# One shared home for the last weight pieces and sixteen 8-byte loads at the end of the load queue: a decode step of attention plus MLP

## The chip, the cores and the metric

The kernel runs on one core of one Trainium2 chip. A core has TensorE (PE, matmuls), VectorE (DVE), ScalarE (ACT), GpSimd (POOL), SyncE (SP, which here only issues transfers) and 16 DMA engines that move data between device memory (HBM) and the core's on-chip memory (SBUF). SBUF has 128 partitions. The matmuls add up in a second on-chip memory, PSUM. A transfer is issued on the queue of an engine (here SP, ACT or POOL), carried out by DMA engines, and reports by a semaphore that it has landed.

The metric is device time in microseconds (us), the median over runs without the profiler. The profile shows one further execution. Its span, from the first to the last instruction, is a little shorter than the device time of that execution.

## The reference

One token `x` (1 × 1024) is normalised; attention with 32 query heads on 4 cached key/value heads of 65,536 positions each, and a small MLP, are added to it. All is bf16.

```python
def reference(A_x, A_k_cache, A_v_cache, A_wq, A_wo, B_x, B_w1, B_w2, B_w3, B_w4):
...
    x = A_x
    xn = _layernorm(x, axis=-1)
    return x + _A_ref(xn, A_k_cache, A_v_cache, A_wq, A_wo) + _B_ref(xn, B_w1, B_w2, B_w3, B_w4)
```

`_A_ref` is `softmax(q kᵀ / sqrt(128)) v`, projected by `wo` (4096 × 1024), with `q = xn wq` and `wq` 1024 × 4096. `_B_ref` normalises `xn` again and uses four weights: `h = gelu(layernorm(xn) w1)`, four quarters of `h` shifted along a sequence (which has one position here, so that the shifted values are all outside it), `x1 = xn + hs w2`, and `x1 + gelu(layernorm(x1) w3) w4`, where `w3` is 1024 × 3584 and `w4` 3584 × 1024. The two caches have 64 MiB each; the kernel reads 170 MB in all.

## The kernel before, in words

**Items.** All that is large is cut into 47 items (lines 82 to 91), each loaded by one transfer on SP's queue and used by one compute function. In order: `wq` in two halves; for each of four key/value heads `g` and each of four rounds `r` a tile of K and a tile of V (16,384 positions, 4 MiB each), with `w3` (two halves) and `w1` put in between, and `wo` of that head after its rounds; then `w2`; then `w4` in five pieces. `W4_PIECES` (line 19) is (16, 8, 2, 1, 1): 16, 8, 2, 1 and 1 of the 28 chunks of 128 rows that w4 has, so 4096, 2048, 512, 256 and 256 KB. In the text the five are called piece 0 to piece 4.

**Slots.** The pool `big` (line 61) holds five slots of 128 partitions × 32 KiB. `slot()` (line 95) takes the next one in rotation, so that an item lies where the item five places earlier lay, and its load waits until that item has landed and has been read for the last time. `issue` (line 98) takes a slot, picks the source and issues the load (line 118). `ensure` (line 129) issues items up to a number, and the main loop (lines 440 to 442) keeps the issues `LOOKAHEAD` = 4 items ahead of the computing. For the last items this means: piece 0 takes the slot of V of the last round but one, piece 1 that of K of the last round, piece 2 that of V of the last round, piece 3 that of the last `wo`, and piece 4 that of `w2`.

**Computing.** `compute_K` transposes a K tile in place on DVE (line 353), multiplies it with the queries on PE (line 357) and makes softmax weights of a round on DVE and ACT. `compute_V` multiplies the weights with the V tile on PE (line 389). `group_end` joins the four rounds of a head, and `compute_wo` projects the head. Everything that ends in the output is added up in one PSUM bank, `psB`, by `row_acc` (line 160): two rows of 512 sums, from `x`, `wo`, `w2` and `w4`.

**The end.** `compute_w4` (line 326) adds each piece to `psB`, two matmuls for each chunk: 32, 16, 4, 2 and 2. After the last piece ACT copies the first 256 columns of `psB` to SBUF (line 336) and DVE the other 256 (line 337); two stores of 1 KB each bring them to HBM, one on ACT's queue (line 339), one on SP's (line 340). Each engine issues its own instructions in the order of the program; when the instruction at the head waits, what is behind it waits too.

**Semaphores.** The framework gives each transfer that SP or ACT issues one of eight completion semaphores, in rotation over both queues. A transfer that takes a semaphore which an earlier transfer has used is issued only when that earlier transfer is known to have landed. The framework adds a wait in front of the issue where the program doesn't imply it anyway. At the end of the program SP waits for all eight.

Of the kernel before, what the change touches and what calls it, by code (L numbers as in the profile page):

```python
# [8 lines left out]
BF16 = mybir.dt.bfloat16  # L9
# [9 lines left out]
W4_PIECES = (16, 8, 2, 1, 1)  # L19
# [3 lines left out]
def kernel(  # L23
# [14 lines left out]
    nc = tc.nc  # L38
# [11 lines left out]
    NOUT = A_wo.shape[1]  # L50
# [8 lines left out]
    const = ctx.enter_context(tc.tile_pool(name="const", bufs=1))  # L59
# [20 lines left out]
    w4_start = [sum(W4_PIECES[:i]) for i in range(len(W4_PIECES))]  # L80

    items = [("wq", 0), ("wq", 1)]
# [10 lines left out]
    st = {}  # L93

    def slot():
        return big.tile([P, KEYS], BF16, name="slot")

    def issue(item):
        kind = item[0]
        t = slot()  # L100
        if kind == "wq":
            src = wq_v[:, 4 * item[1]:4 * item[1] + 4, :].rearrange("p c n -> p (c n)")
        elif kind == "w3":
            src = w3_v[:, 4 * item[1]:4 * item[1] + 4, :].rearrange("p c n -> p (c n)")
        elif kind == "w4":
            c0 = w4_start[item[1]]
            src = w4_v[:, c0:c0 + W4_PIECES[item[1]], :].rearrange("p c n -> p (c n)")
        elif kind == "w1":
            src = w1_v
        elif kind == "w2":  # L110
            src = w2_v
        elif kind == "wo":
            src = wo_v[item[1]]
        else:
            cache = A_k_cache if kind == "K" else A_v_cache
            _, g, r = item
            src = cache[0, g, r * KEYS:(r + 1) * KEYS, :].rearrange("(p k) d -> p (k d)", p=P)
        nc.sync.dma_start(out=t[:, 0:src.shape[-1]], in_=src)
        st[item] = t
# [7 lines left out]
    n_issued = [0]  # L127

    def ensure(upto):
        while n_issued[0] <= min(upto, len(items) - 1):  # L130
            issue(items[n_issued[0]])
            n_issued[0] += 1
# [85 lines left out]
    for cg in range(4):  # L218
        nc.vector.tensor_copy(out=selbig[:, cg, :].rearrange("p (hl dd) -> p hl dd", dd=16),
                              in_=sel32[:, 8 * cg:8 * cg + 8].unsqueeze(2).to_broadcast([P, 8, 16]))  # L220
    sel8big = const.tile([P, P], F32, name="sel8big")
    nc.vector.tensor_copy(out=sel8big[:].rearrange("p (hl dd) -> p hl dd", dd=16),
                          in_=sel8[:].unsqueeze(2).to_broadcast([P, 8, 16]))
# [3 lines left out]
    for b in range(2):  # L227
        for par in range(2):
            nc.vector.tensor_copy(out=psel[:, 2 * b + par, :].rearrange("p (a i) -> p a i", a=4),  # L229
                                  in_=iv[:, b, par, :].unsqueeze(1).to_broadcast([P, 4, 32]))  # L230
# [200 lines left out]
    def compute_wo(g):  # L431
        wt = st.pop(("wo", g))[:, 0:8 * NOUT].rearrange("p (j n) -> p j n", n=NOUT)
        oT5 = st.pop(("oT5", g))
        for j in range(8):
            for h2 in range(2):
                row_acc(h2, oT5[:, j:j + 1], wt[:, j, 512 * h2:512 * (h2 + 1)])

    compute = {"wq": compute_wq, "w3": compute_w3, "w1": compute_w1, "w2": compute_w2, "w4": compute_w4,
               "wo": compute_wo, "K": compute_K, "V": compute_V}
    for i, it in enumerate(items):  # L440
        ensure(i + LOOKAHEAD)
        compute[it[0]](*it[1:])


# [28 lines left out]
```

## Time and profile before

| what | value |
|---|---|
| median of 3 runs | 406.52 us (406.5 to 406.79) |
| the profiled execution, device time | 406.69 us |
| its span | 404.8 us |
| mean granted TensorE clock | 0.796 |
| PE busy | 245.7 us (61%) |
| DVE busy | 215.7 us (53%) |
| ACT busy | 37.7 us (9%) |
| read from HBM | 169.88 MB, 420 GB/s over the span |

The profile page divides the span into 40 equal slices and gives, as a digit in tenths, the busy share of each engine and of the 16 DMA engines together. Other views of the same trace list the instructions in order of time, what an engine waited for, the busy time in chosen stretches, the transfers with the time from issue to landing, and the chain of waits: from the last instruction back to what released it, and so on. A line such as `L118` is line 118 of the kernel. `SPq` and `ACTq` are the issuing instructions of SP and ACT; `PEld` is the loading of weights into PE. `x5` counts instructions, and `a<-b` says that `a` is written from `b`.

### The profile page before, as it was taken

What the parts mean: (1) busy time and instruction counts of PE and PEld (TensorE: products, weight loads), DVE (VectorE), ACT (ScalarE), POOL (GpSimd) and SP (SyncE); (2) the same over time, 40 slices, a digit from 0 to 9 for tenths busy, and PEclk for the clock granted to TensorE, in tenths of its full rate; (3) what the DMA queues carried; (4) which work ended last, traced back from release to release, by engine and by line L of the source; (5) the groups of instructions that cost most, each with busy time, mean ns of one, the idle gap of its engine ahead of it and who ended that gap; (6) DMA issues with size and microseconds to landing.
All of it is one profiled execution on the core that took longest, in us unless ns stands there. A gap on an engine that the chain in (4) does not pass through costs nothing.

```text
span 404.8 us, 3326 instructions
## 1 busy us (share of the span) xinstructions
PE 245.7 (61%) x1400; PEld 95.7 (24%) x1400; DVE 215.7 (53%) x235; ACT 37.7 (9%) x60; POOL 11.2 (3%) x30
## 2 busy tenths in 40 slices
PE   0385565328475847557657948384659474758456
PEld 0132222103132312112223313131233121213122
DVE  0419474017484848346665847475748383838500
ACT  0101101100201010120210010101010101010100
POOL 5001000000000000000010000000000000000000
PEclk9998878857795778768595868888958797679898
DMA  8999999999999999999999999999999999999993
GB/s 363 415 424 449 418 426 434 430 418 444 434 408 439 447 416 419 458 418 416 447 431 413 437 444 414 435 440 418 430 440 424 428 439 427 425 437 413 440 415 134
DMA packets 7065, 170.11 MB, mean 420 GB/s; under 512 B 1023, under 2 KB 1033, under 8 KB 1418
## 3 DMA queue, kind: packets, MB, share of 16 engines
q1 hardware_dynamic: 6772, 169.87, 98.0%
q8 instruction: 11, 0.18, 0.2%
q0 software_dynamic: 128, 0.02, 0.0%
q10 hardware_dynamic: 150, 0.01, 0.0%
q14 instruction: 4, 0.03, 0.0%
HBM read 169.88 MB, written 0.01 MB: 420 GB/s over the span
## 4 chain that ended last, share of the span: by engine, by line
DMA 54%; PE 23%; DVE 17%; ACT 2%; another core or an unknown queue 1%; issue 1%; DVEq 0%; ACTq 0%
DMA slot<-in_A_k_cache_dram 44%; DVE slot L353 11%; PE sc L357 10%; DMA slot<-in_B_w_dram 7%; PE psB L160 5%; PE oacc L389 4%; DMA x_bf<-in_A_x_dram 3%; DVE pT L377 2%; DVE mx L361 2%; ACT p_sb L374 2%; PE rows L244 1%; PE pm_e L417 1%; DVE m L365 0%; PE pm_mx L363 0%
## 5 line engine op out<-in xcount | busy, mean ns | idle before, releaser
L353 DVE STREAM_TRANSPOSE slot<-slot 128x2048 f32<-128x2048 f32 x64 | 142.3, 2281 | 61.1 <-DMA slot<-in_A_k_cache_dram 61.1
L357 PE MATMUL sc<-slot,qst 128*128 128x512 bf16 x512 | 131.6, 411 | 40.9 <-DVE slot L353 40.9
L389 PE MATMUL oacc<-slot,pT 128*32 128x512 bf16 x512 | 56.0, 616 | 48.0 <-DVE pT L377 48.0
L357 PEld LDWEIGHTS <-qst 128*128 128x128 bf16 x512 | 51.6, 103 | 125.1 <-issue 45.9
L361 DVE TENSOR_REDUCE mx<-sc 128x1 f32<-128x1024 f32 x16 | 19.6, 1225 | 34.7 <-PE sc L357 34.7
L374 ACT ACTIVATE p_sb<-sc,nball 128x1024 bf16<-128x1024 f32 x16 | 17.8, 1114 | 209.8 <-DVE nball L372 209.8
L389 PEld LDWEIGHTS <-pT 128*32 128x32 bf16 x512 | 17.5, 139 | 75.0 <-DVE pT L377 49.4
L377 DVE STREAM_TRANSPOSE pT<-p_sb 128x1024 bf16<-128x1024 bf16 x16 | 19.9, 1245 | 23.3 <-ACT p_sb L374 23.3
L244 PE MATMUL rows<-slot,xpad 128*32 128x512 bf16 (+1 forms) x144 | 13.6, 509 | 6.1 <-DMA slot<-in_B_w_dram 6.1
L363 PE MATMUL pm_mx<-ident_f,mx 128*1 128x128 f32 x16 | 4.3, 270 | 21.1 <-DVE mx L361 21.1
L160 PE MATMUL psB<-slot,oT 128*1 128x512 bf16 x64 | 12.6, 564 | 4.3 <-DVE oT L428 4.3
L394 ACT COPY ob<-oacc 128x512 f32<-128x512 f32 x12 | 7.0, 586 | 58.6 <-PE oacc L389 58.6
L160 PE MATMUL psB<-slot,dst_h 128*1 128x512 bf16 x56 | 7.9, 444 | 3.2 <-DMA slot<-in_B_w_dram 3.2
L370 PE MATMUL pm_mx<-ident_f,rep 1*128 1x1 f32 x16 | 3.5, 222 | 9.9 <-DVE rep L367 9.9
L417 PE MATMUL pm_e<-og,selbig 128*128 128x128 f32 x32 | 7.4, 403 | 3.4 <-DVE og L409 3.4
L244 PEld LDWEIGHTS <-xpad 128*32 128x32 bf16 x144 | 5.7, 127 | 15.0 <-issue 13.7
L172 PE MATMUL pm_ln<-ln_rowsum_a,ones_f 128*128 128x1 f32 x2 | 0.6, 348 | 13.6 <-DVE psel L229 13.6
L337 DVE CAST out<-psB 64x256 bf16<-64x256 f32 x1 | 0.4, 417 | 15.2 <-ACT out L336 15.2
L363 PEld LDWEIGHTS pm_mx<-ident_f,mx 128*1 128x1 f32 x16 | 1.3, 79 | 29.0 <-DVE mx L361 29.0
L417 PEld LDWEIGHTS pm_e<-og,selbig 128*128 128x128 f32 x32 | 6.3, 293 | 6.7 <-DVE og L409 6.7
L365 DVE TENSOR_REDUCE m<-pm_mx 1x8 f32<-1x128 f32 x16 | 4.4, 278 | 5.8 <-PE pm_mx L363 5.8
L374 ACT ACT_TABLE_LOAD x3 | 3.8, 1283 | 35.6 <-DVE nball L372 35.6
(97 smaller groups left out, 79.3 us busy)
## 6 DMA issues: line engine op xcount, KB each, us to landing
slot<-in_A_k_cache_dram SPq DMA_DIRECT2D x16, 4096.0 KB, 34.5
slot<-in_A_v_cache_dram SPq DMA_DIRECT2D x16, 4096.0 KB, 35.5
slot<-in_A_wq_dram SPq DMA_DIRECT2D x2, 4096.0 KB, 21.4
slot<-in_A_wo_dram SPq DMA_DIRECT2D x4, 2048.0 KB, 38.4
slot<-in_B_w_dram SPq DMA_DIRECT2D x2, 3584.0 KB, 42.6
slot<-in_B_w_dram SPq DMA_DIRECT2D x3, 2048.0 KB, 26.9
slot<-in_B_w_dram SPq DMA_DIRECT2D x1, 4096.0 KB, 27.8
slot<-in_B_w_dram SPq DMA_DIRECT2D x1, 512.0 KB, 16.1
```

The source lines that it names most:

```text
L160: nc.tensor.matmul(psB[32 * j:32 * j + 1, :], lhsT=lhsT, rhs=rhs, start=(not row_started[j]), stop=False, tile_position=(0, 32 * j), skip_ ...
L244: nc.tensor.matmul(acc[32 * j:32 * j + 32, bk, 0:width], lhsT=xp[:, c, :], rhs=wt[:, cl, ch * width:(ch + 1) * width], start=(c == 0), sto ...
L353: nc.vector.transpose(out=kf[:, cg, :], in_=kf[:, cg, :])
L357: nc.tensor.matmul(sc[:, hf, :], lhsT=qst[g % 2][:, o:o + 128], rhs=kr[:, cg, hf, :, bp // 2, :, bp % 2], start=(cg == 0 and bp == 0), sto ...
L361: nc.vector.reduce_max(out=mx[:], in_=sc[:].rearrange("p h n -> p (h n)"), axis=AX.X)
L363: nc.tensor.transpose(pm[0:1, 0:P], mx[:, 0:1], ident_f[:])
L365: nc.vector.reduce_max(out=m8[:], in_=pm[0:1, 0:P].rearrange("o (j h) -> o h j", h=8), axis=AX.X)
L374: nc.scalar.activation(out=p_sb[:], in_=sc[:], func=ACTF.Exp, bias=nball[:, r:r + 1], scale=SCALE, accum_out=lall[:, r:r + 1])
L377: nc.vector.transpose(out=pT[:], in_=p_sb[:])
L389: nc.tensor.matmul(oacc[32 * u:32 * (u + 1), :], lhsT=pT[:, hf, 32 * t:32 * (t + 1)], rhs=vt[:, :, hf, t, :], start=(hf == 0 and t < 4), s ...
L394: nc.scalar.copy(out=ob[:], in_=oacc[:])
L417: nc.tensor.matmul(pe[:, 0:P], lhsT=selbig[:, cg, :], rhs=og[:, 128 * cg:128 * (cg + 1)], start=(cg == 0), stop=(cg == 3))
```

## The change

Two things are changed. In `issue`, pieces 1 to 4 of w4 take one slot together: piece 1 takes it from the rotation, and pieces 2 to 4 lie behind it in the same slot, each in its own columns. As soon as piece 1 has been issued, the main loop issues the rest. And a new small tile `probe` (16 partitions, 16 × 4 elements of bf16) is filled by sixteen loads on SP's queue, issued after piece 4: the k-th reads 4 elements (8 bytes) of `A_x` for each of k partitions. Nothing reads `probe`. The computing is the same, and so is the order of all other instructions on the other engines.

```diff
@@ -97,7 +97,14 @@
     def issue(item):
         kind = item[0]
-        t = slot()
+        if kind == "w4" and item[1] > 0:
+
+            if item[1] == 1:
+                st["w4home"] = slot()
+            a = (w4_start[item[1]] - w4_start[1]) * NOUT
+            t = st["w4home"][:, a:a + W4_PIECES[item[1]] * NOUT]
+        else:
+            t = slot()
         if kind == "wq":
...
@@ -437,8 +444,17 @@
+
+    probe = const.tile([16, 16, 4], BF16, name="probe")
+    xv = A_x[0, 0, :].rearrange("(p c) -> p c", c=32)
     for i, it in enumerate(items):
         ensure(i + LOOKAHEAD)
+        if n_issued[0] > len(items) - len(W4_PIECES) + 1:
+            ensure(len(items))
+        if n_issued[0] == len(items):
+            n_issued[0] += 1
+            for k in range(1, 17):
+                nc.sync.dma_start(out=probe[0:k, k - 1, :], in_=xv[0:k, 0:4])
         compute[it[0]](*it[1:])
```

In the built program the sixteen loads stand on SP's queue between the load of piece 4 and the store of line 340 (line 347 after the change); the loads are line 457 after the change, and the item loads line 125.

## The prediction

> **What bounds the kernel now.** I read the page's slices first, then the tail by stretches of a microsecond or more, then the chain of waits from 380 us on, and last the issues on the queues of SyncE (SP) and ScalarE (ACT), one by one. The page's slices:
>
> ```profile
> DMA  8999999999999999999999999999999999999993
> q1 hardware_dynamic: 6772, 169.87, 98.0%
> ```
>
> The 16 DMA engines are busy in every slice but the first and the last, almost all of it on q1, the queue that SP feeds: the kernel streams 170 MB of cache and weights, and the stream sets the time. Only the tail, where the stream runs out, can answer to this change. The stretches around it (PE, PEld, DVE, ACT, POOL busy, then granted clock, DMA share, GB/s):
>
> ```profile
> 384.60:394.70 10.10, 5.85 (x49) 2.58 (x49) 0.94 (x4) 0.00 (x0) 0.00 (x0) 0.91 0.97 416
> 394.70:397.00 2.30, 2.30 (x17) 0.79 (x14) 0.00 (x0) 0.00 (x0) 0.00 (x0) 0.65 0.96 382
> 397.00:398.00 1.00, 1.00 (x14) 0.35 (x10) 0.00 (x0) 0.00 (x0) 0.00 (x0) 1.00 0.62 232
> 400.00:401.00 1.00, 0.99 (x10) 0.27 (x6) 0.00 (x0) 0.00 (x0) 0.00 (x0) 1.00 0.02 8
> ```
>
> The DMA engines are full to 397 us, then run dry one after another until 400.7. The chain of waits (start, length, what):
>
> ```profile
> 365.42 27.79 DMA slot<-in_B_w_dram
> ...
> 393.26 7.49 PE psB L160 x54
> ...
> 400.76 0.40 PE psB L160 x2
> ...
> 401.18 0.38 ACT out L336
> ...
> 401.57 0.42 DVE out L337
> ```
>
> w4's first piece lands at 393.2, PE works through the pieces as they land, its last pair of matmuls starts at 400.76, two copies bring the sums out of PSUM, and two stores (L339 on ACT, L340 on SP) end it. Sizes and times to landing of the last two pieces, issued at 388.38 and 390.11:
>
> ```profile
> slot<-in_B_w_dram SPq DMA_DIRECT2D x1, 256.0 KB, 11.7
> slot<-in_B_w_dram SPq DMA_DIRECT2D x1, 256.0 KB, 10.6
> ```
>
> So they land at 400.08 and 400.71; by the same sum the pieces before them land at 393.2, 398.2 and 399.4. The last landing releases the last pair. What one issue takes of its queue:
>
> ```profile
> 1.66 0.43 SPq L118 DMA_DIRECT2D slot<-in_A_k_cache_dram  x1
> 390.11 0.33 SPq L118 DMA_DIRECT2D slot<-in_B_w_dram  x1
> 402.02 0.63 SPq L340 DMA_DIRECT2D out_dram<-out  x1
> 0.75 0.42 ACTq L123 DMA_DIRECT2D x_bf<-in_A_x_dram  x1
> 1.20 0.54 ACTq L125 DMA_DIRECT2D x_row_bf<-in_A_x_dram  x1
> 401.57 0.61 ACTq L339 DMA_DIRECT2D out_dram<-out  x1
> ```
>
> A transfer over 128 partitions takes 0.33 us alone and 0.42 to 0.43 back to back at the start; one over two rows (the stores) 0.61 to 0.63, one over one row (L125) 0.54. Consecutive issues stand 0.05 us apart (1.66 + 0.43, and the next at 2.13). Behind SP's store:
>
> ```profile
> SPq L468 <- DMA out_dram<-out: 0.9, 2, 0.5
> ```
>
> SP waits twice at most 0.5 us for the two stores; the first of these waits ends at 403.2, so ACT's store lands 1.6 us after its issue at 401.57. From SP's store at 402.02 to the end of the span at 404.8 lie 2.8 us, the same whatever starts it.
>
> **The change, part by part.** *One home for pieces 1 to 4.* Only piece 1 still waits for a slot, as before (K of the last round read by PE, 374.86). Pieces 2, 3 and 4 lose their waits and go out some 0.38 us apart behind it, by 376.4, where they went out at 383.30, 388.38 and 390.11. What it gains: nothing, because their data stand behind the same bytes on engines that are 0.97 and 0.96 busy until 397; a later tail has no bytes that could start earlier. Bounds: if the last piece did land sooner, the last pair could start sooner by at most the 0.3 us for which the weight loads stood idle before 400.76; a loss has no mechanism, as the order of the bytes is unchanged. I take 0. The matmuls, copies and ACT's store stay where they are.
>
> *Sixteen loads on SP, in front of L340.* Their 136 runs of 8 bytes stand behind all weights on the engines, so the bytes cost nothing. Their place in SP's queue does. The built program's instruction list shows eight completion semaphores that hardware DMAs use in turn, and that each load first waits for the previous user of its semaphore. Load 1 waits for V of the last round, 2 for wo, 3 for w2, 4 for w4's piece 0, 5 for piece 1; piece 2's semaphore goes to ACT's store; load 6 waits for piece 3, 7 for piece 4, loads 8 to 12 for loads 1 to 5, **load 13 for ACT's store**, 14 to 16 for loads 6 to 8, and SP's store for load 9. Loads 1 to 5 go out under the stream, the fifth at about 398.3, on a queue that was idle there. Load 6 can't go before 400.08 nor load 7 before 400.71; behind load 7 ten issues and then the store stand on SP, and the store used to go at 402.02. Nothing else is queued on SP; ACT's store waits only for piece 2, landed at 399.4.
>
> The price of one such issue, d, has no row: 7 to 15 partitions lie between the store's 2 (0.63) and the loads' 128 (0.33). Lower bound 0.33 for all. Upper bound, flat at the store's 0.63 for all but load 16, which alone has as many partitions as there are DMA engines and which I give 0.33 throughout (0.3 more if that is wrong). A straight line from 0.63 at 2 to 0.33 at 16 gives 0.44 at 11, the middle of loads 7 to 15. Between line and flat I take 0.54, which is also the row over one partition.
>
> [...]
>
> Sum with d = 0.54: load 6 at 400.12 to 400.66; load 7 at 400.75; loads 7 to 15 are 9 × (0.54 + 0.05) = 5.3, to 406.06; load 16 0.38, to 406.44; SP's store at 406.45 instead of 402.02, **4.4 us later**. Load 13 comes at 404.3, past ACT's landing at 403.2, so that wait is covered; without the cover (d small) it decides. With landings 1.6 us after issue, as of ACT's store, loads 6 to 9 (out by 402.5) have landed by 404.1, before 14 to 16 and the store ask. Span 404.8 + 4.4 = 409.2. This execution took 406.69, 0.17 above the median 406.52; the 1.9 us around the span stay. Predicted median 406.52 + 4.4 = **410.9**.
>
> Bounds: d = 0.63: load 7 at 400.78, 9 × 0.68 + 0.38 = 6.5, store at 407.28, +5.3, 411.8. d = 0.33: six issues from 400.75 end at 403.03; load 13 waits to 403.22, four issues of 0.38, store at 404.74, +2.7, **409.2**.
>
> **The rivals.** (1) *Small loads issue like large ones*, and ACT's store is the new wait: 409.2. For it: most issues of the trace cost 0.33. Against: all three rows under 16 partitions cost 0.54 or more. [...]
> (2) *Landings bind*: tiny transfers land late, and loads 14 to 16 and the store wait for loads 6 to 9. The four small transfers issued by POOL took 6.5 to 7.3 us to land. With 6.5, load 9, out at 401.9, lands at 408.4, and the store goes then: +6.4, 412.9. Against: those ran under a full stream; after 400.7 the engines are empty, and the stores took 1.6.
> (3) *Cost grows with the partitions*: ACT's rows are 0.54 at one and 0.61 at two; 0.07 for each further one gives a mean of 1.24 for loads 7 to 15 and 0.89 for load 6, store at 413.0, +11, 417.5. Against: the 128-partition transfer is the cheapest row.
> (4) *Not slower*: the semaphore waits are satisfied while the stream still runs, all sixteen loads are issued between 376.4 and 393 on a queue that is idle there, and the store keeps its 402.02. It decides if the last wait falls before 402.02 − 11 × 0.59 = 395.5. Time 406.2 to 406.5 (the 0.3 of the earlier pieces at most). For it: SP has nothing else to issue from 376.4 on. Against: loads 6, 7 and 13 are listed as waiting for transfers that land at 400.1, 400.7 and 403.2. That the change doesn't do what it says has this same time.
>
> **How the numbers follow.** Forecast (SP's issues end the kernel, d of about 0.45 to 0.65) 0.65; rival 1 0.15; rival 2 0.07; rival 3 0.09; rival 4 0.04. The range goes from a little under rival 1 to a little over rival 2, 408.8 to 413.2, and leaves out rivals 3 and 4. About 0.2% (0.8 us) is what a measurement of this kernel can tell from no change. Only rival 4 isn't slower: slower 0.96, same 0.03, faster 0.01.
>
> **What would show it.** SP's queue after 400 us would have some ten issues of 0.5 to 0.6 us with no gap, and the store at about 406.4; pieces 2 to 4 issued by 376.5 and PE's last pair still within 0.3 us of 400.76; ACT's store still at 401.6. A gap ahead of load 13 that ends with ACT's store is rival 1; gaps ahead of 14 to 16, rival 2; issue lengths that rise along the sixteen, rival 3. The prediction is wrong if the loads are issued before 400, or if their issue costs lie outside 0.33 to 0.63.

## The result and the profile after

The changed kernel takes **408.86 us** (median of 3 runs, 408.75 to 409.26) against 406.52: 2.34 us or 0.6% slower, ratio 1.0058, 95% interval 1.0035 to 1.0081. Its profiled execution took 408.75 with a span of 407.0. In what follows line numbers of the changed kernel are 7 higher from line 100 to the main loop than before; the small loads are line 457, and SP's store is line 347.

The slices of the page, as shown of before:

```profile
DMA  9999999999999999999999999999999999999991
q1 hardware_dynamic: 7044, 169.87, 97.4%
```

The stream is the same 169.87 MB, and the last slice, which ends at 407.0, is emptier. The stretches around the tail (PE, PEld, DVE, ACT, POOL busy, granted clock, DMA share, GB/s):

```profile
384.60:394.70 10.10, 6.63 (x61) 3.05 (x61) 0.93 (x4) 0.00 (x0) 0.00 (x0) 1.00 0.96 410
394.70:397.00 2.30, 1.48 (x14) 0.53 (x11) 0.00 (x0) 0.00 (x0) 0.00 (x0) 1.00 0.91 358
397.00:398.00 1.00, 0.53 (x6) 0.26 (x7) 0.00 (x0) 0.00 (x0) 0.00 (x0) 1.00 0.57 209
400.00:401.00 1.00, 0.39 (x4) 0.08 (x1) 0.15 (x1) 0.37 (x1) 0.00 (x0) 1.00 0.01 0
```

The stream does not run out later. It runs out sooner, as the chain of waits says (start, length, what):

```profile
374.51 22.92 DMA slot<-in_B_w_dram
...
400.03 0.40 PE psB L167 x2
...
400.45 0.38 ACT out L343
...
400.85 0.42 DVE out L344
```

The last pair of matmuls starts at 400.03 instead of 400.76, and everything up to DVE's copy is 0.7 us earlier than before. The time is lost behind it, on SP's queue (start, length, what, count):

```profile
374.51 1.75 SPq L125 DMA_DIRECT2D slot<-in_B_w_dram  x4
400.01 4.05 SPq L457 DMA_DIRECT2D probe<-in_A_x_dram  x10
401.73 0.48 SPq L457 DMA_DIRECT2D probe<-in_A_x_dram  x1
402.48 0.31 SPq L457 DMA_DIRECT2D probe<-in_A_x_dram  x1
404.15 0.60 SPq L347 DMA_DIRECT2D out_dram<-out  x1
```

The first row is pieces 1 to 4 of w4, issued together by 376.3. The second is loads 7 to 16, from the landing of the last piece on; the third and the fourth are two of them, load 12 and load 13. Load 12 ends at 402.21, load 13 starts at 402.48, and SP's own list of waits gives the reason for the gap:

```profile
SPq L457 <- DMA out_dram<-out: 0.3, 1, 0.3
```

It is the store on ACT's queue, issued at 400.85 and landed 1.6 us later:

```profile
400.85 0.61 ACTq L346 DMA_DIRECT2D out_dram<-out  x1
```

SP's store goes 404.15 − 400.01 = 4.14 us after the last piece has landed (load 7, which waits for that landing, starts at 400.01); before, it went 402.02 − 400.71 = 1.31 us after. That is 2.8 us more, of which 0.7 is hidden by the stream's earlier end, and the span grows by 2.2. Two questions follow: what the 2.8 consist of, and where the 0.7 come from.

### The profile page after: what moved, and what is told of

Same layout as the page of the kernel before. It is cut to its first block, busy times and chain, and to the rows that moved or that the text cites. A ratio compares the mean times of both kernels' runs of the same rounds, so it can differ in the third digit from the quotient of the medians.

```text
span 407.0 us, 3340 instructions
## 1 busy us (share of the span) xinstructions
PE 243.9 (60%) x1400; PEld 93.5 (23%) x1400; DVE 215.7 (53%) x235; ACT 37.7 (9%) x60; POOL 11.2 (3%) x30
## 2 busy tenths in 40 slices
DMA packets 7337, 170.11 MB, mean 418 GB/s; under 512 B 1295, under 2 KB 1305, under 8 KB 1690
## 3 DMA queue, kind: packets, MB, share of 16 engines
q1 hardware_dynamic: 7044, 169.87, 97.4%
## 4 chain that ended last, share of the span: by engine, by line
DMA 60%; PE 20%; DVE 14%; ACT 2%; another core or an unknown queue 1%; issue 1%; DVEq 0%; ACTq 0%
DMA slot<-in_A_k_cache_dram 52%; PE sc L364 12%; DVE slot L360 9%; DMA slot<-in_B_w_dram 6%; DMA x_bf<-in_A_x_dram 3%; PE oacc L396 3%; PE psB L167 2%; PE rows L251 2%; DVE pT L384 1%; DVE mx L368 1%; ACT p_sb L381 1%; ACT L190 0%; DVE m L372 0%; PE pm_e L424 0%
## 5 line engine op out<-in xcount | busy, mean ns | idle before, releaser
L364 PE MATMUL sc<-slot,qst 128*128 128x512 bf16 x512 | 135.1, 422 | 42.4 <-DVE slot L360 42.3
L364 PEld LDWEIGHTS <-qst 128*128 128x128 bf16 x512 | 52.8, 105 | 128.6 <-issue 50.2
L167 PE MATMUL psB<-slot,dst_h 128*1 128x512 bf16 x56 | 6.5, 378 | 3.7 <-DMA slot<-in_B_w_dram 3.7
L424 PE MATMUL pm_e<-og,selbig 128*128 128x128 f32 x32 | 4.6, 288 | 3.4 <-DVE og L416 3.4
L416 DVE SCALAR_TENSOR_TENSOR og<-oacc,wts,og 128x512 f32<-128x512 f32 x4 | 3.0, 750 | 6.3 <-PE oacc L396 6.3
```

What stands on the lines that cost most here:

```text
L167: nc.tensor.matmul(psB[32 * j:32 * j + 1, :], lhsT=lhsT, rhs=rhs, start=(not row_started[j]), stop=False, tile_position=(0, 32 * j), skip_ ...
L364: nc.tensor.matmul(sc[:, hf, :], lhsT=qst[g % 2][:, o:o + 128], rhs=kr[:, cg, hf, :, bp // 2, :, bp % 2], start=(cg == 0 and bp == 0), sto ...
L424: nc.tensor.matmul(pe[:, 0:P], lhsT=selbig[:, cg, :], rhs=og[:, 128 * cg:128 * (cg + 1)], start=(cg == 0), stop=(cg == 3))
```

## The experiments

| run | median, us | ratio to before, 95% interval |
|---|---|---|
| the change | 408.86 | 1.0058 (1.0035 to 1.0081) |
| home | 406.60 | 1.0001 (0.9992 to 1.0010) |
| loads | 409.02 | 1.0060 (1.0047 to 1.0074) |
| eight | 406.06 | 0.9989 (0.9980 to 0.9997) |
| twelve | 407.06 | 1.0015 (1.0006 to 1.0024) |
| all2 | 408.62 | 1.0052 (1.0039 to 1.0064) |
| pad128 | 406.02 | 0.9987 (0.9978 to 0.9996) |
| pad32 | 404.55 | 0.9952 (0.9938 to 0.9965) |
| pad64 | 406.56 | 0.9999 (0.9991 to 1.0008) |
| pad96 | 406.19 | 0.9993 (0.9984 to 1.0001) |
| pad160 | 406.02 | 0.9988 (0.9979 to 0.9997) |
| change_aligned | 407.28 | 1.0019 (1.0010 to 1.0028) |

The kernel before had medians of 406.53 to 406.58 beside these runs.

**The two parts alone.** `home` keeps the shared slot and leaves the small loads out:

```diff
-    probe = const.tile([16, 16, 4], BF16, name="probe")
-    xv = A_x[0, 0, :].rearrange("(p c) -> p c", c=32)
...
-        if n_issued[0] == len(items):
-            n_issued[0] += 1
-            for k in range(1, 17):
-                nc.sync.dma_start(out=probe[0:k, k - 1, :], in_=xv[0:k, 0:4])
```

> The shared home alone, without the sixteen loads. Theory (the loads' place on SP's queue is the whole loss, the bytes of the last pieces cannot come sooner): as before within 0.3 us, pieces 2 to 4 issued by 376, the last pair of matmuls within 1 us of 400.4 in the profile. Rival (the earlier issue ends the stream sooner, and the 0.7 us by which the last piece landed sooner in the profile of after is its gain): 0.5 to 0.8 us faster than before.

406.60, no difference. Pieces 1 to 4 go out together at 374.51, as in the change, and the last pair of matmuls starts 0.07 us before that of the kernel before, by the chain of waits of `home`:

```profile
400.69 0.40 PE psB L167 x2
```

So the shared home gains nothing, and the 0.7 us aren't its work. Nor are they the work of the granted clock in that profile: from 394.70 to 397.00 it was 1.00 in `home` as in the change, against 0.65 before, and the last pair still starts at 400.69. `loads` is the other half, the same loads after a load order as before:

> The sixteen loads alone, pieces 2 to 4 in slots of their own as before. Theory: the loads alone carry the loss, +2.3 to +2.9 us against before, with SP's store 4.1 us after the last piece has landed. Rival (the shared home gains 0.5 to 0.8, the loads cost 2.9 to 3.1): 0.5 us or more slower than the whole change. Second rival (pieces 2 to 4 and the loads only hurt together): within 0.5 us of before.

409.02, +2.48: the loads alone carry the loss. The first rival wanted 0.5 us or more above the change; it is 0.16, and the runs of the two overlap. The last pair of matmuls of `loads` starts early as in the change, though the pieces wait for their slots again:

```profile
400.12 0.40 PE psB L160 x2
```

The early end goes with the loads, then, or with something that comes with them.

**Fewer loads.** `eight` and `twelve` change only the count; here `eight`, and `twelve` has `range(1, 13)`:

```diff
-            for k in range(1, 17):
+            for k in range(1, 9):
```

> The change with eight loads in place of sixteen. Theory: loads 6 to 8 are issued by 0.9 us after the last piece has landed, before DVE's copy ends 1.3 us after it, so SP's store goes as before: 0 to +0.2 us against before. Rival (each load costs its share of the loss, 2.3/16 = 0.15 us): +1.2 us.

> The change with twelve loads: now it is SP's own store that takes the semaphore of ACT's store, and waits for its landing. Theory: loads 6 to 12 end 2.2 us after the last piece has landed, ACT's store lands 2.5 us after it, SP's store goes at 2.55 in place of 1.3: +1.2 us against before. Theory without that wait (issue time on SP alone): the store at 2.3, +1.0. Rival of equal shares: 12 x 0.15 = +1.8 us.

`eight` took 406.06: SP's queue behaves as the theory says, and the time is still not the one it gave, but 0.5 us below before. SP's issues of `eight`:

```profile
399.92 1.25 SPq L457 DMA_DIRECT2D probe<-in_A_x_dram  x3
401.85 0.60 SPq L347 DMA_DIRECT2D out_dram<-out  x1
```

The three loads end at 401.17, and the store goes at 401.85 as soon as DVE's copy is done: they cost nothing. (The profiled execution took 406.44, the longest of the eleven.) `twelve` took 407.06, +0.52 in place of the +1.2 expected. There SP's own store has the semaphore of ACT's store; SP's issues, then its wait:

```profile
399.59 2.84 SPq L457 DMA_DIRECT2D probe<-in_A_x_dram  x7
402.74 0.60 SPq L347 DMA_DIRECT2D out_dram<-out  x1
```

```profile
SPq L347 <- DMA out_dram<-out: 0.3, 1, 0.3
```

The store goes 402.74 − 400.22 = 2.52 us after the last landing (load 7's start), as expected (2.55). The time alone can't tell the two theories of `twelve` apart, +1.2 and +1.0; the wait in the line above does. In both runs the queue is right and the total that the theory gives is 0.5 to 0.7 too high: some gain is missing from the theory, and it does not depend on the number of loads.

**The missing gain.** The changed kernel has one more tile, `probe`, among the constants: 128 bytes per partition. The pools behind the constants, the five slots among them, lie 128 bytes further. `pad128` is the kernel before with an unused tile of that size in that place, and no loads:

```diff
+    pad = const.tile([P, 64], BF16, name="pad")
+    nc.gpsimd.memset(pad[:], 0.0)
     for i, it in enumerate(items):
```

> Before, with an unused tile of 128 bytes per partition in the place of the tile that the loads fill (set to zero once, on POOL), so that the five slots and all pools behind them lie at the same addresses as in the changed kernel: 128 bytes further. No loads, no shared home. Theory (the 0.5 us by which the kernels with loads end sooner than their delays add up to is the place of the slots): 0.4 to 0.6 us faster than before, last piece landed about 0.5 sooner. Rival (it comes from the loads themselves or their instructions): within 0.15 us of before.

406.02: 0.56 us faster than before, with nothing done but this. Its last pair of matmuls starts 0.74 us earlier than before, which is the early end of the change (the two profiled executions lie 0.73 apart, 405.96 and 406.69, the medians 0.56):

```profile
400.02 0.40 PE psB L160 x2
```

Against `pad128` the delays fit the theories: `eight` +0.04, `twelve` +1.04, the change +2.84, `loads` +3.00. `pad32` has `[P, 16]`, which is 32 bytes, in its place, and so puts the slots at multiples of 512 bytes:

> The same with 32 bytes, which puts the slots at multiples of 512 bytes. If the place of the slots matters by its alignment: at least as fast as with 128 bytes, 0.5 to 1.5 us faster than before. If any shift does it: as with 128 bytes. If the place does not matter: within 0.15 us of before.

404.55, 2.0 us faster than before, more than the 0.5 to 1.5 expected, and the fastest kernel of this study. The end of its chain of waits, and its queue of large loads:

```profile
396.03 2.87 PE psB L160 x24
...
399.31 0.42 DVE out L337
```

```profile
q1 hardware_dynamic: 6772, 169.87, 98.1%
```

DVE's last copy starts 2.26 us earlier than before (401.57), on the same packets and bytes. The packets themselves are shorter: 98.1% of 402.6 us is 395.0 us of each DMA engine, where before 98.0% of 404.8 is 396.7. The records of single packets in the two traces say it more finely: in `pad32` 99% of the packets of 32 KB took 1213 ns, before only 16% did, and most of the others took 1214 to 1224. Three more sizes were to tell which multiple counts:

> Before with an unused tile of 64 bytes per partition at the end of the constants: slots at 32 bytes past a multiple of 512 (480 past before, 96 past in the changed kernel, 0 past with the 32-byte tile). If a start at a multiple of 64 bytes is what counts: like the 128-byte tile, 0.3 to 0.7 us faster than before. If it is the distance behind the last multiple of 512 or 256: between the two, 0.6 to 2 us faster.

> The same with 96 bytes: slots at 64 bytes past a multiple of 512. If a multiple of 64 is what counts: as fast as with the 32-byte tile, 1.8 to 2.2 us faster than before. If it must be a multiple of 128, 256 or 512: 0.3 to 1 us faster.

> The same with 160 bytes: slots at 128 bytes past a multiple of 512. Multiple of 64 or of 128: 1.8 to 2.2 us faster than before. Multiple of 256 or 512: 0.3 to 1 us faster.

| slots start, bytes past a multiple of 512 | 0 | 32 | 64 | 96 | 128 | 480 (before) |
|---|---|---|---|---|---|---|
| median, us | 404.55 | 406.56 | 406.19 | 406.02 | 406.02 | 406.53 |
| all packets of the trace, us for each of 16 engines | 396.1 | 397.9 | 397.6 | 397.5 | 397.6 | 397.8 |

A multiple of 64 or of 128 isn't enough: 64 and 128 gain 0.3 and 0.5 (the interval of 64 just includes no gain), 0 gains 2.0. `pad64` was to gain under either reading and gains nothing; it too has an added tile that is set to zero, so that this setting is not what gains. Whether a start at a multiple of 256 that isn't one of 512 would do was not tried. One trace bears on it: in `forms` (below) the slots start 320 bytes past a multiple of 512, which is 64 past one of 256. Its packets of 32 KB took 1215, 1213 and 1222 ns most often (1830, 896 and 706 of 4480), as those of `pad96`, at 64, did (1873, 849 and 732). Other starts have other times: 1214, 1213 and 1218 ns most often at 96, in the change (1127, 1053 and 587 of 4480), and 1216, 1224 and 1213 at 480, before (1989, 788 and 729). This speaks for 256 as the period, by one profile.

Other pools move with the slots, so that the runs do not show that it is the slots alone; the shorter packets speak for them, as the slots take nearly all the bytes (the queue of large loads moved 169.87 of 170.11 MB before).

`change_aligned` is the whole change with a further unused tile of 416 bytes, slots at a multiple of 512:

> The whole change with a further unused tile of 416 bytes, so that the slots lie at multiples of 512 bytes. Theory (the loads cost the same 2.8 us whatever the stream does, and the two effects add): 2.0 us faster than with the slots at 37856, plus 2.8: 407.2 to 407.6, 1.4 us faster than the change. Rival (the gain of the place is lost when SP's queue ends the kernel): 408.7 to 409.0.

407.28, as the theory had it. Against `pad32` that is +2.73: the loads cost the same on a faster stream.

**The wait for ACT's store.** In the change the gap before load 13 is only 0.27 us. `all2` makes the issues shorter, two partitions in every load, so that the wait would have to grow if it is one:

```diff
-                nc.sync.dma_start(out=probe[0:k, k - 1, :], in_=xv[0:k, 0:4])
+                nc.sync.dma_start(out=probe[0:2, k - 1, :], in_=xv[0:2, 0:4])
```

> The change with sixteen loads of two partitions each, whose issue took 0.24 us in the profile of after. Theory (load 13 waits for ACT's store, four issues follow): issue is done sooner, the wait before load 13 grows from 0.27 to 0.7 us, SP's store goes 3.6 us after the last landing in place of 4.16: 0.5 us faster than the whole change. Without that wait (issue time alone): store at 2.9, 1.3 us faster than the whole change.

408.62. The saving is 0.24 us of the median, half of the 0.5 expected; issue time alone would have given 1.3. SP's store goes 403.92 − 400.14 = 3.78 us after the last landing, where 3.6 was expected. Loads 12 and 13, SP's store, and SP's wait for ACT's store:

```profile
401.60 0.25 SPq L457 DMA_DIRECT2D probe<-in_A_x_dram  x1
402.70 0.23 SPq L457 DMA_DIRECT2D probe<-in_A_x_dram  x1
403.92 0.60 SPq L347 DMA_DIRECT2D out_dram<-out  x1
```

```profile
SPq L457 <- DMA out_dram<-out: 0.8, 1, 0.8
```

The wait has grown to 0.8 us, and load 13 still starts 402.70 − 400.14 = 2.56 us after the last landing (2.47 in the change): what the shorter issues save ahead of it is waited away.

**What an issue costs.** `forms` is the kernel before with sixteen small transfers on SP in the middle of the stream, two of each form, each directly behind the load of an item:

```diff
+    forms = [load_2x512, load_2x8, load_16x8, load_1x256, load_128x16, store_2x512_apart, store_2x512, store_2x8]
     for i, it in enumerate(items):
         ensure(i + LOOKAHEAD)
+        if 8 <= i < 40 and i % 2 == 0:
+            n = (i - 8) // 2
+            forms[n % 8](n)
```

> Before, with sixteen small transfers on SP in the middle of the stream, two of each of eight forms, to see what the issue of each form costs. Theory (it is the direction, a store into HBM, that makes an issue cost 0.6): the three forms of store about 0.6 whatever their size, the five of load 0.24 to 0.4. Rival (it is the 512 bytes of a run): loads of two runs of 512 bytes 0.6, stores of two runs of 8 bytes 0.25. Rival (it is the source rows 32 partitions apart): only the store of such rows 0.6.

One run, for the profile alone. The instructions by the tile they touch, in ns (min/median/max); `la` to `le` are the five loads in the order of the list, `sa` the store of two rows that lie 32 partitions apart, as in the kernel's own stores, `sb` the same with adjacent rows, `sc` adjacent rows of 8 bytes:

```profile
L458 SPq DMA_DIRECT2D lb<-in_A_x_dram x2: 283/284/284, 111.6 to 252.0; - x2
L462 SPq DMA_DIRECT2D lc<-in_A_x_dram x2: 423/428/432, 129.3 to 271.7; - x2
L470 SPq DMA_DIRECT2D le<-in_A_x_dram x2: 426/426/426, 164.1 to 307.3; - x2
L474 SPq DMA_DIRECT2D sa<-psel x2: 496/532/567, 175.7 to 324.5; - x2
L478 SPq DMA_DIRECT2D sb<-psel x2: 283/284/284, 199.8 to 343.6; - x2
```

The theory (a store costs 0.6) falls, and so does the rival of the 512 bytes: `la`, a load of two such runs, took 0.28 and 0.33. A store of two adjacent rows costs 0.28 us, as does a load of two; the same store from rows 32 partitions apart costs 0.50 to 0.57. Among loads the number of partitions counts: 0.28 for two, 0.43 for sixteen and for 128. A load of one row of 256 bytes (`ld`) took 0.28 and 0.29.

## Why the prediction came out as it did

*What bounds the kernel, and the shared home at nothing*: right in the main. `home` shows 406.60, and pieces 2 to 4 were issued by 376.3 as said. But that only the tail can answer to this change was wrong, as the last point below shows, and so was the bound of 0.3 us on an earlier last pair: it came 0.7 us earlier.

*The order on SP's queue and its waits*: right, load by load. Loads 1 to 5 vanish under the stream, load 7 goes as the last piece lands, ten issues stand between that landing and SP's store, nothing waits ahead of loads 14 to 16, and the store's delay is passed on whole (404.15 to 407.0 is 2.85 us; before, 2.78).

*The price of an issue, d = 0.54*: this is the step that failed. It meets a sign of being wrong that the prediction had named, issue costs outside 0.33 to 0.63: the sixteen took 0.24 to 0.48 us, with a median of 0.30:

```profile
L457 SPq DMA_DIRECT2D probe<-in_A_x_dram x16: 235/300/484, 376.3 to 403.7; - x16
```

Loads 7 to 16 fill 4.05 us with the gap of 0.27 ahead of load 13 and eight gaps of about 0.045: 0.34 each, where the forecast had 0.54 for nine and 0.33 for one. It took the price from SP's own store and from a one-row load at the start, and read those rows as the price of few partitions. `forms` shows that the store is dear for its rows 32 partitions apart, and that few partitions make an issue cheaper: the sixteenth load, given the lowest price, took 0.39, the second 0.24. What made the one-row load at the start take 0.54 stays open; `ld`, also one row, took 0.28 and 0.29. So does the 0.48 of load 12, which stands out between 0.33 and 0.31. No run shows the 0.33 that load 16 was given for its sixteen partitions: it took 0.39, and a load of sixteen took 0.42 to 0.43 in `forms`, as did one of 128. Nor does any show a flat 0.63 below sixteen: loads 1 to 15 took 0.24 to 0.48.

*"That wait is covered"*: wrong as a consequence. With cheap issues SP reaches load 13 before ACT's store has landed, and waits. This is rival 1 as it was priced: the store 404.74 − 400.71 = 4.03 us after the last landing, +2.7; measured 4.14 us and, with the slots in the same place, +2.84. Rivals 2 and 4 have nothing for them. Of rival 3 a trace is left: 0.24 at two partitions, 0.39 at sixteen, 0.01 for each and not 0.07.

*What no case held*: the new tile moves the slots by 128 bytes, and that alone gains 0.56 us (`pad128`). The forecast looked for effects of `probe` on SP's queue and in the bytes, not in the addresses behind it. 406.52 − 0.56 + 2.83 (the store's further delay in the profile, 4.14 − 1.31) is 408.79, and the median is 408.86.

That 408.86 lies just inside the stated range, which begins at 408.8, doesn't speak for the forecast's own mechanism. The low end had been set for rival 1, which was given a chance of 0.15, and it was luck that the 0.56 us that nobody had reckoned with, pulling the same way as the cheaper issues, did not carry the time below it.

## What to carry to other kernels

A transfer that nobody reads still holds its place in its queue, and where a framework gives completion semaphores in rotation, it can also be made to wait for a transfer of another queue (here sixteen such loads cost 2.84 us with the slots in the same place, and the wait took 0.3 us of SP's queue, 0.8 in `all2`): list the waits of the built program, and look at what stands between the last landing and the last store. Price an issue by a row with the same shape on both sides, not by one that only has the same number of rows: two rows cost 0.28 us or 0.50 to 0.57 in `forms`. In a kernel bound by its loads, look at where the tiles they fill begin: an unused tile of 32 bytes, which put the slots at multiples of 512, made this one 0.5% faster than the kernel before.

## What the runs showed of the hardware that was not expected

The start of the slots within 512 bytes moved the time by up to 2.0 us of 406.5, and not in proportion to the distance from the multiple below: 32 and 480 bytes past are the slowest (406.56 and 406.53), 64 to 128 past in between (406.02 to 406.19), 0 by far the fastest (404.55). What 32 and 480 have in common is that both lie 32 bytes from the nearest multiple; off the multiple, the starts nearest to it are the slowest.

The sources in HBM stayed and only the places written to moved. Why 32 bytes past loses as much as 480, these runs do not say.

The rows of a store's source matter for its issue: 0.28 us adjacent, 0.50 to 0.57 at 32 partitions apart, for the same two runs of 512 bytes. And the same load of 128 partitions took 0.33 us alone (piece 4 before) but 0.42 to 0.43 directly behind another (pieces 2 to 4 in the changed kernel: four issues in 1.75 us).
